# Pooled attention feeding a routed MoE: k and v read a batch further ahead, and all batches in one hand-ordered part

## The chip, the cores and the metric

One core of one Trainium2 chip runs the whole program. The metric is device microseconds for one execution; every number in the trace is in microseconds from the start of the profiled span unless it is marked ns. Engines are named as in the profile: PE (matmul), PEld (its weight load), DVE, ACT, POOL, and SP, which here issues DMAs and reads registers.

## The reference

Eight batches, eight heads, 576 tokens, head width 64. k and v are averaged over groups of 8 tokens (72 groups), then ordinary attention follows, and its output is the input of a mixture of experts with 4 groups of 4 experts, top 1 in each.

```python
k_p = k.reshape(B, H, Sp, 8, D).mean(axis=3)          # B=8 H=8 S=576 D=64, Sp=72
v_p = v.reshape(B, H, Sp, 8, D).mean(axis=3)
attn = softmax(q @ k_p.T / sqrt(D))                   # (B, H, S, 72)
x = (attn @ v_p).transpose(0, 2, 1, 3).reshape(4608, 512)
g_idx = argmax(x @ w_group); g_w = softmax(...)[g_idx]           # 4 groups
e_idx = argmax(x @ w_expert[g_idx]); e_w = softmax(...)[e_idx]   # 4 experts in the group
out[tok] = g_w * e_w * (relu(x[tok] @ w1[g, e]) @ w2[g, e])      # w1 512x1024, w2 1024x512
```

## The kernel before, in words

Work goes batch by batch. For each batch the kernel finds the expert that most of its tokens chose ("main expert"), and runs all 576 tokens through it; tokens of other experts are left to a loop behind the last batch. Products run in fp32r with both operands split into a high and a low half, so each up and each down product is three matmul passes. A batch has 16 up products (`m.up:f:half`, line 577, eight slices of the hidden width by two halves of the tokens, 12 matmuls each) and 14 pieces of down products (`m.down:z`, lines 606 and 617, 8 matmuls of 512 columns each).

Three batches are in flight. While batch b (`m`) runs its products, attention of b + 1 (`n`) and the pooling of b + 2 (`x`) are threaded between them. What the pieces do that matter here:

- `load_k`, `load_v` (lines 199 and 228): the reads of k and v of one batch from HBM, 1.31 MB each, on SP's queue, into the tiles `kv` and `vv`. Each of these has one buffer, so a read waits until the folds of the batch before have read it. v of the last batch goes in six DMAs instead of four, two of which overlap.
- `kr:0`, `kr:1` (line 263): k folded by sums over 8 tokens, on DVE, in place in `kv`, result in `kb`. `vr:0`, `vr:1` (line 282): the same for v on Pool, result in `v6`; `vm` (line 288) adds two short Pool operations.
- `load_qb` (line 255): q, 16 DMAs of small pieces on SP.
- `route`, `main_expert` (lines 427, 462): DVE finds the expert; SP reads its number into a register (line 475) and can only then issue `w.load` (line 541), four reads of 512 KB for w1 of the next batch. `w.load:2`, `m.load:2` are w2's. Tiles `sw` have four buffers.
- `cast` (ACT, line 554) makes a weight's high half, `lo` (Pool, line 560) the low half.
- `keep_x` (line 520): the attention output is stored to HBM where tokens are left over.
- LAST, the plan of the last batch, also places the left-over tokens (`l.step`, class Left). Its first step makes a triangle on Pool, copies it and a tile of ones on ACT (lines 691, 692), and has PE multiply with them (line 707).

The order of these pieces is written out by hand: START and FIRST (batch 0), SECOND (batch 1), STEADY (batches 2 to 6) and LAST (batch 7) are lists of pieces, and `run` calls them one after the other. Inside `tc.manual_schedule` each engine gets its instructions in the order of the calls. In the kernel before there is one such part for START, FIRST and SECOND, and one for each later batch. Where two parts meet, a scheduler merges their streams engine by engine.

The last batch begins:

```python
LAST = """
m.load:2:3 m.lo:1:2:v l.step l.step m.load:2:2 m.up:0:0 m.up:0:1 m.upd:0:1 m.upd:0:0 p.tail l.step ...
```

```python
nc.gpsimd.affine_select(out=tri, in_=ones, ...)
nc.scalar.copy(out=trir, in_=tri)      # line 691
nc.scalar.copy(out=onesr, in_=ones)    # line 692
...
nc.tensor.matmul(ps[:, 0:n], lhsT=lhs, rhs=lf[:, o:o + n], start=True, stop=True)   # line 707
```

Of the kernel before, what the change touches and what calls it, by code (L numbers as in the profile page):

```python
# [17 lines left out]
B, H, S, D = 8, 8, 576, 64  # L18
# [33 lines left out]
m.up:0:0 m.upd:0:0 n.qb:0 m.up:1:0 m.upd:1:0 m.split:1:2:p:2 m.load:2:2 a.count n.kt m.up:0:1 m.upd:0:1 a.keep_x m.split:1:3:p:2 m.load:2:3 m.up:1:1 m.upd:1:1 n.sc:0 n.mx:0 n.sb:0 n.qb:1 m.up:2:0 m.upd:2:0 n.su_:0 n.nm:0:p m.split:2:0:p:2 m.up:2:1 m.upd:2:1 n.sc:1 n.mx:1 n.sb:1 n.pt:0 n.qb:2  # L52
x.load_v m.up:3:0 m.upd:3:0 n.su_:1 n.nm:1:p m.split:2:1:p:2 m.up:3:1 m.upd:3:1 m.up:4:0 m.upd:4:0 n.sc:2 n.mx:2 n.sb:2 n.pt:1 n.qb:3 x.load_k m.split:2:2:p:2 m.up:4:1 m.upd:4:1 n.su_:2 n.nm:2:p m.up:5:0 m.upd:5:0 m.up:5:1 m.upd:5:1 n.sc:3 n.mx:3 n.sb:3 n.pt:2 n.qb:4
x.load_qb:0 x.load_qb:1 x.load_qb:2 x.load_qb:3 m.up:6:0 m.upd:6:0 n.su_:3 n.nm:3:p m.up:7:0 m.upd:7:0 n.av:0 n.avd:0 m.split:2:3:p:2 m.up:6:1 m.upd:6:1 n.sc:4 n.mx:4 n.sb:4 n.pt:3 m.up:7:1 m.upd:7:1 n.su_:4 n.nm:4:p m.down:0 n.pt:4 x.vr:0 m.down:1 x.vr:1 x.vm m.down:2 m.store:0 m.down:3 n.av:1 n.avd:1
m.down:4 x.kr:0 n.rt:0 n.rt:1 m.down:5 m.store:1 n.route_g n.route_e:p x.kr:1 m.down:6 m.down:7 x.qb:0 m.down:8 m.store:2 x.kt n.main_expert w.load:1:0 w.load:1:1 w.load:1:2 w.load:1:3 n.gates n.gm_ n.keep_x m.down:9 w.split:1:0:p:2 w.load:2:0
x.sc:0 x.mx:0 x.sb:0 m.down:10 x.qb:1 m.down:11 m.store:3 w.split:1:1:p:2 w.load:2:1 x.su_:0 x.nm:0:p m.down:12 w.cast:1:2 m.down:13 m.store:4 w.cast:1:3
"""
STEADY = """
m.up:0:0 p.tail m.upd:0:0 n.sc:1 n.pt:0 m.lo:1:2 m.load:2:2 m.up:0:1 n.mx:1 m.upd:0:1 m.up:1:0 n.sd:1 m.lo:1:3 m.load:2:3 m.upd:1:0 n.ex:1 m.up:1:1 m.cast:2:0 m.upd:1:1 n.su_:1 n.nm:1:p
m.up:2:0 m.upd:2:0 n.qb:2 m.lo:2:0 x.load_k x.load_v m.up:2:1 m.upd:2:1 n.pt:1 m.up:3:0 n.sc:2 m.upd:3:0 m.cast:2:1 m.lo:2:1 n.mx:2 m.up:3:1 m.upd:3:1 n.sd:2  # L60
m.up:4:0 m.upd:4:0 n.ex:2 m.up:4:1 m.upd:4:1 n.su_:2 n.nm:2:p x.load_qb:0 x.load_qb:1 m.up:5:0 m.upd:5:0 m.cast:2:2 m.lo:2:2 m.up:5:1 m.upd:5:1 n.pt:2
x.load_qb:2 x.load_qb:3 m.up:6:0 m.upd:6:0 m.up:7:0 m.cast:2:3 m.lo:2:3 m.upd:7:0 n.av:0 n.avd:0 m.up:6:1 m.upd:6:1
m.up:7:1 m.upd:7:1 n.av:1 n.rt:0 n.avd:1
m.down:0 n.rt:1 x.kr:0 m.down:1 x.kr:1 m.down:2 n.route m.down:3 m.down:4 m.down:5 n.main_expert w.load:1:0 w.load:1:1 w.load:1:2 w.load:1:3
x.qb:0 n.gates n.gm_ n.keep_x m.down:6 x.vr:0 x.kt m.down:7 x.sc:0 x.mx:0 x.sd:0 w.cast:1:0 w.lo:1:0 w.load:2:0 m.down:8 x.ex:0 x.qb:1 w.cast:1:1 w.load:2:1 m.down:9
x.su_:0 x.nm:0:p w.lo:1:1 m.down:10 x.vr:1 x.vm m.down:11 m.down:12 w.cast:1:2 m.down:13 w.cast:1:3
"""
LAST = """
m.load:2:3 m.lo:1:2:v l.step l.step m.load:2:2 m.up:0:0 m.up:0:1 m.upd:0:1 m.upd:0:0 p.tail l.step l.step l.step m.up:1:0 m.up:1:1 m.upd:1:0
# [7 lines left out]
MANUAL = {ET.PE, ET.SP, ET.DVE, ET.Activation, ET.Pool}  # L77

@with_exitstack
def attn_moe(ctx: ExitStack, tc: tile.TileContext, q, k, v, wg, we, w1, w2, out):  # L80
# [840 lines left out]
                nc.tensor.matmul(ps[:, 0:256], lhsT=ones, rhs=ones.unsqueeze(1).broadcast_to([128, 2, 128]), start=True, stop=True)  # L921

    left, top = Left(), Top()
    att = [Att(b) for b in range(B)] + [None] * 2
    moe = [Moe(a) if a else None for a in att]

    def run(plan, b):

        who = dict(a=att[b], m=moe[b], n=att[b + 1], w=moe[b + 1], p=moe[b - 1] if b else None, x=att[b + 2] if b + 2 < B else None, t=top, l=left)
        for piece in plan.split():  # L930
            name, *args = piece.split(":")
            who_, fn = name.split(".")
            if who[who_] is not None:
                getattr(who[who_], fn)(*[int(z) if z.isdigit() else z for z in args])

    with tc.manual_schedule(engines=MANUAL):
        run(START, 0)
        run(FIRST, 0)
        run(SECOND, 1)
    for b in range(2, B):  # L940
        with tc.manual_schedule(engines=MANUAL):
            run(LAST if b == B - 1 else STEADY, b)

    nit = nc.values_load(left.niti[0:1, 0:1], min_val=0, max_val=B * (NE + S // BS))
# [31 lines left out]
```

## Time and profile before

| what | value |
|---|---|
| median of 3 runs | 516.83 us (516.13 to 522.19) |
| profiled execution, its own time | 517.89 us |
| its span | 516.2 us |
| granted TensorE clock, mean | 0.998 of full speed |
| busy: PE, PEld, DVE, ACT, POOL | 503.1, 445.3, 328.7, 206.8, 255.2 us |
| DMA | 83.74 MB, mean 162 GB/s |

The span is the profiled program from its first to its last instruction; the execution's own time has about 1.7 us around it. Busy times of different engines overlap. A matmul's end is modelled, so a high busy share of PE says that it seldom stood still, not that every matmul ran at its best pace. An idle time of an engine is put down to the instruction of another engine that ended it; "issue" stands for a time in which the engine waited for nothing that the profile shows. DMA share is the mean busy share of 16 DMA engines and can come out slightly above 1 in short stretches.

### The profile page before, as it was taken

What the parts mean: (1) busy time and instruction counts of PE and PEld (TensorE: products, weight loads), DVE (VectorE), ACT (ScalarE), POOL (GpSimd) and SP (SyncE); (2) the same over time, 40 slices, a digit from 0 to 9 for tenths busy, and PEclk for the clock granted to TensorE, in tenths of its full rate; (3) what the DMA queues carried; (4) which work ended last, traced back from release to release, by engine and by line L of the source; (5) the groups of instructions that cost most, each with busy time, mean ns of one, the idle gap of its engine ahead of it and who ended that gap; (6) DMA issues with size and microseconds to landing.
All of it is one profiled execution on the core that took longest, in us unless ns stands there. A gap on an engine that the chain in (4) does not pass through costs nothing.

```text
span 516.2 us, 14897 instructions
## 1 busy us (share of the span) xinstructions
PE 503.1 (97%) x6085; PEld 445.3 (86%) x6085; DVE 328.7 (64%) x927; ACT 206.8 (40%) x385; POOL 255.2 (49%) x235
## 2 busy tenths in 40 slices
PE   8799999999999999999999999999999999989996
PEld 7698977998789988898889988898889988889876
DVE  6887877888376765485654766385664763268702
ACT  2454342454226441645235542454325551344212
POOL 2394766565418722785049641685138850422400
PEclk9999999999999999999999999999999999999999
DMA  8699299395248942788155961997345200743741
GB/s 278 191 272 195 54 265 258 76 241 108 52 131 247 244 77 103 225 244 139 28 198 162 249 90 44 336 336 134 56 150 196 76 2 20 237 160 123 265 165 57
DMA packets 118126, 83.74 MB, mean 162 GB/s; under 512 B 71034, under 2 KB 93818, under 8 KB 117800
## 3 DMA queue, kind: packets, MB, share of 16 engines
q1 hardware_dynamic: 113424, 75.70, 54.8%
q10 hardware_dynamic: 4600, 7.02, 3.9%
q8 instruction: 49, 0.80, 0.7%
q14 instruction: 21, 0.17, 0.1%
q0 software_dynamic: 32, 0.04, 0.0%
HBM read 77.31 MB, written 28.53 MB: 205 GB/s over the span
## 4 chain that ended last, share of the span: by engine, by line
PE 75%; DVE 9%; DMA 5%; POOL 3%; ACT 2%; issue 2%; SPq 1%; ACTq 1%; DVEq 0%; POOLq 0%
PE mm L577 29%; PE mm L606 26%; PE mm L617 4%; PE sc L393 4%; PE sc L333 3%; PE tp L411 3%; POOL w L560 2%; DMA sw<-in_moe_w_dram 2%; DMA vv<-in_v_dram 2%; DMA out_dram<-y 1%; PE mm L638 1%; DVE pT L379 1%; DVE s L365 1%; DVE ht L590 1%; DVE p L354 1%
## 5 line engine op out<-in xcount | busy, mean ns | idle before, releaser
L606 PE MATMUL mm<-w,ht 128*128 128x512 f32 x744 | 171.9, 384 | 0.0
L560 POOL TENSOR_TENSOR w<-sw,w 128x1024 fp32r<-128x1024 f32 (+2 forms) x87 | 148.9, 1729 | 43.5 <-ACT w L554 43.4
L606 PEld LDWEIGHTS mm<-w,ht 128*128 128x128 f32 x744 | 136.9, 189 | 21.1 <-issue 1.6
L577 PE MATMUL mm<-xb,w 128*128 128x288 f32 (+1 forms) x768 | 109.7, 295 | 1.0 <-issue 1.0
L577 PEld LDWEIGHTS mm<-xb,w 128*128 128x128 f32 x768 | 100.7, 189 | 5.7 <-ACT w L554 2.2
L577 PE MATMUL mm<-xa,w 128*128 128x288 f32 (+1 forms) x768 | 100.8, 284 | 3.0 <-DVE ht L590 1.4
L577 PEld LDWEIGHTS mm<-xa,w 128*128 128x128 f32 x768 | 95.5, 190 | 5.2 <-ACT ht L579 1.7
L579 ACT ACTIVATE ht<-mm 128x288 fp32r<-128x288 f32 (+2 forms) x128 | 51.9, 410 | 89.8 <-PE mm L577 88.1
L554 ACT CAST w<-sw 128x1024 fp32r<-128x1024 f32 x64 | 66.7, 1041 | 27.3 <-DMA sw<-in_moe_w_dram 24.5
L372 POOL TENSOR_TENSOR p<-p,su 128x864 f32<-128x864 f32 (+2 forms) x30 | 40.3, 1344 | 68.5 <-DVE su L367 53.3
L590 DVE SCALAR_TENSOR_TENSOR ht<-mm,ht 128x64 fp32r<-128x64 f32 (+4 forms) x192 | 37.7, 251 | 31.7 <-ACT ht L579 31.6
L611 ACT ACTIVATE y<-mm,gm 128x512 f32<-128x512 f32 x31 | 21.3, 686 | 68.1 <-PE mm L606 67.4
L512 POOL TENSOR_TENSOR mp<-oh,moh 128x80 f32<-128x80 f32 x8 | 2.9, 356 | 84.9 <-DVE moh L477 81.5
L359 ACT ACTIVATE p<-p 128x864 f32<-128x864 f32 (+2 forms) x30 | 23.4, 781 | 37.5 <-DVE p L354 29.8
L379 DVE STREAM_TRANSPOSE pT<-p 128x960 f32<-128x960 f32 (+2 forms) x30 | 29.2, 972 | 8.4 <-POOL p L372 7.8
L585 DVE SCALAR_TENSOR_TENSOR ht<-mm,ht 128x288 fp32r<-128x288 f32 (+1 forms) x64 | 27.0, 422 | 10.4 <-ACT ht L579 10.4
L365 DVE TENSOR_REDUCE s<-p 128x12 f32<-128x864 f32 (+2 forms) x30 | 25.8, 860 | 8.3 <-ACT p L359 8.3
L617 PE MATMUL mm<-w,ht 128*128 128x512 f32 x128 | 29.6, 381 | 0.0
L333 PEld LDWEIGHTS sc<-kT,qT 64*32 64x32 f32 x2176 | 23.7, 105 | 6.4 <-issue 3.5
L333 PE MATMUL sc<-kT,qT 64*32 64x72 f32 x2176 | 28.5, 230 | 0.5 <-DVE qT L319 0.3
L345 DVE TENSOR_REDUCE mx<-sc 128x12 f32<-128x864 f32 (+2 forms) x28 | 24.3, 868 | 5.5 <-PE sc L333 5.5
L393 PE MATMUL sc<-pT,v 32*64 32x288 f32 (+2 forms) x384 | 27.0, 409 | 0.2 <-DVE p L354 0.2
(213 smaller groups left out, 533.6 us busy)
## 6 DMA issues: line engine op xcount, KB each, us to landing
sw<-in_moe_w_dram SPq DMA_DIRECT2D x72, 512.0 KB
vv<-in_v_dram SPq DMA_DIRECT2D x27, 320.0 KB
q<-in_q_dram SPq DMA_DIRECT2D x112, 72.0 KB
kv<-in_k_dram SPq DMA_DIRECT2D x14, 512.0 KB
out_dram<-y ACTq DMA_DIRECT2D x23, 256.0 KB
xscr<-xa SPq DMA_DIRECT2D x5, 1152.0 KB
xscr<-xb SPq DMA_DIRECT2D x5, 1152.0 KB
pT<-xscr SPq DMA_DIRECT2D x4, 1152.0 KB
```

The source lines that it names most:

```text
L333: nc.tensor.matmul(ps[x][32 * g:32 * g + 32, SP * t:SP * t + SP], lhsT=s.qT[c][64 * x:64 * x + 64, g, 32 * t:32 * t + 32], rhs=s.kT[64 * x ...
L365: red(out=two[:, :, :, 0], in_=p.rearrange("p t (x s) -> p t x s", x=2), axis=AX.X, op=ALU.add)
L372: (nc.vector if eng == "v" else nc.gpsimd).tensor_tensor(out=p, in0=p, in1=bc(s.su[c][:, 0:w], SP), op=ALU.mult)
L379: nc.vector.transpose(out=s.pT[:, :, o:o + n].rearrange("p j (t i) -> p t j i", i=32), in_=probs[:, z:z + n // 32].rearrange("p t (j i) -> ...
L393: nc.tensor.matmul(banks[a][64 * x:64 * x + 64, 0:n], lhsT=s.v6[32 * a:32 * a + 32, 5 if x and i == 0 else j, :], rhs=s.pT[32 * a:32 * a + ...
L554: nc.scalar.copy(out=s.w[m, j][0], in_=raw)
L560: (nc.vector if eng == "v" else nc.gpsimd).tensor_tensor(out=wl[:, i:i + n], in0=s.raw[m, j][:, i:i + n], in1=wh[:, i:i + n].bitcast(F32), ...
L577: nc.tensor.matmul(ps[:, 0:n], lhsT=l[:, kc, fs], rhs=apart(s.a.xt[hf][:, r, kc]), start=(kc == 0 and i == 0), stop=(kc == 3 and i == 2))
L579: nc.scalar.activation(out=halves(ht[:, sl]), in_=joined(ps[:, 0:n]), func=AF.Relu)
L590: stt(out=ht[:, at:at + hi - lo], in0=ps[:, a, lo:hi], scalar=0.0, in1=ht[:, t + lo:t + hi].bitcast(F32), op0=ALU.max, op1=ALU.subtract)
L606: nc.tensor.matmul(ps, lhsT=s.ht[f][:, 640 * l + o:640 * l + o + 128], rhs=apart(s.w[2, f // 2][r][:, f % 2, :]), start=(i == 0), stop=(i ...
L617: nc.tensor.matmul(ps, lhsT=s.ht[f][:, 512:640], rhs=apart(s.w[2, f // 2][r][:, f % 2, :]), start=(i == 0), stop=(i == 15))
```

## The change

Two things change. First, the reads of k and v move a batch further ahead. A new letter `z` stands for batch b + 3 (`att` gets one more empty place at its end). In STEADY `x.load_k x.load_v` leave up product 2, and `z.load_v z.load_k` stand behind `x.kr:1` at the second piece of the down products; since `vv` has one buffer, Pool's `x.vr:0`, `x.vr:1` and `x.vm` move from the pieces 6 and 10 of the down products to their beginning, ahead of that read. SECOND gets `z.load_v z.load_k` behind its `x.kr:1`, while its own reads stay. Second, the batches 2 to 7 no longer have a part each: everything from START to LAST is one part.

```diff
 ... SECOND, its fourth line
-m.down:4 x.kr:0 n.rt:0 n.rt:1 m.down:5 m.store:1 n.route_g n.route_e:p x.kr:1 m.down:6 m.down:7 x.qb:0 m.down:8 m.store:2 x.kt n.main_expert w.load:1:0 ...
+m.down:4 x.kr:0 n.rt:0 n.rt:1 m.down:5 m.store:1 n.route_g n.route_e:p x.kr:1 z.load_v z.load_k m.down:6 m.down:7 x.qb:0 m.down:8 m.store:2 x.kt n.main_expert w.load:1:0 ...
 STEADY = """
 m.up:0:0 p.tail m.upd:0:0 n.sc:1 n.pt:0 m.lo:1:2 m.load:2:2 m.up:0:1 n.mx:1 m.upd:0:1 m.up:1:0 n.sd:1 m.lo:1:3 m.load:2:3 ...
-m.up:2:0 m.upd:2:0 n.qb:2 m.lo:2:0 x.load_k x.load_v m.up:2:1 m.upd:2:1 n.pt:1 m.up:3:0 n.sc:2 m.upd:3:0 m.cast:2:1 m.lo:2:1 n.mx:2 m.up:3:1 ...
+m.up:2:0 m.upd:2:0 n.qb:2 m.lo:2:0 m.up:2:1 m.upd:2:1 n.pt:1 m.up:3:0 n.sc:2 m.upd:3:0 m.cast:2:1 m.lo:2:1 n.mx:2 m.up:3:1 ...
...
-m.up:7:1 m.upd:7:1 n.av:1 n.rt:0 n.avd:1
-m.down:0 n.rt:1 x.kr:0 m.down:1 x.kr:1 m.down:2 n.route m.down:3 m.down:4 m.down:5 n.main_expert w.load:1:0 w.load:1:1 w.load:1:2 w.load:1:3
-x.qb:0 n.gates n.gm_ n.keep_x m.down:6 x.vr:0 x.kt m.down:7 x.sc:0 x.mx:0 x.sd:0 w.cast:1:0 w.lo:1:0 w.load:2:0 m.down:8 x.ex:0 x.qb:1 w.cast:1:1 w.load:2:1 m.down:9
-x.su_:0 x.nm:0:p w.lo:1:1 m.down:10 x.vr:1 x.vm m.down:11 m.down:12 w.cast:1:2 m.down:13 w.cast:1:3
+m.up:7:1 m.upd:7:1 n.av:1 n.rt:0 n.avd:1 x.vr:0
+m.down:0 n.rt:1 x.kr:0 x.vr:1 x.vm m.down:1 x.kr:1 z.load_v z.load_k m.down:2 n.route m.down:3 m.down:4 m.down:5 n.main_expert w.load:1:0 w.load:1:1 w.load:1:2 w.load:1:3
+x.qb:0 n.gates n.gm_ n.keep_x m.down:6 x.kt m.down:7 x.sc:0 x.mx:0 x.sd:0 w.cast:1:0 w.lo:1:0 w.load:2:0 m.down:8 x.ex:0 x.qb:1 w.cast:1:1 w.load:2:1 m.down:9
+x.su_:0 x.nm:0:p w.lo:1:1 m.down:10 m.down:11 m.down:12 w.cast:1:2 m.down:13 w.cast:1:3
...
-    att = [Att(b) for b in range(B)] + [None] * 2
+    att = [Att(b) for b in range(B)] + [None] * 3
...
-        who = dict(a=att[b], m=moe[b], n=att[b + 1], w=moe[b + 1], p=moe[b - 1] if b else None, x=att[b + 2] if b + 2 < B else None, t=top, l=left)
+        who = dict(a=att[b], m=moe[b], n=att[b + 1], w=moe[b + 1], p=moe[b - 1] if b else None, x=att[b + 2], z=att[b + 3], t=top, l=left)
...
         run(SECOND, 1)
-    for b in range(2, B):
-        with tc.manual_schedule(engines=MANUAL):
+        for b in range(2, B):
             run(LAST if b == B - 1 else STEADY, b)
```

## Rows read from the trace of the kernel before

**Rows 1.** Busy us of each engine, by stretch: batch 3, last batch (clock, DMA share, GB/s).

```profile
216.45:274.90 58.45, 57.50 (x711) 51.35 (x711) 36.65 (x97) 24.72 (x45) 28.27 (x21) 1.00 0.61 157
...
451.90:516.20 64.30, 58.55 (x500) 52.43 (x498) 33.77 (x119) 19.63 (x36) 13.07 (x16) 0.99 0.45 153
```

**Rows 2.** Waits of PE, then of SP's queue: us in total, times, longest.

```profile
PE mm L577 <- issue: 1.9, 2, 1.0
PE mm L577 <- DVE ht L590: 1.4, 1, 1.4
...
SPq L239 <- DMA vv<-in_v_dram: 9.5, 1, 9.5
```

**Rows 3.** Stretches of 4 us: PE, PEld, DVE, ACT, POOL busy; clock, DMA share, GB/s.

```profile
144.00:148.00 4.00, 4.00 (x23) 3.39 (x22) 3.79 (x9) 1.41 (x4) 0.97 (x1) 1.00 0.01 4
...
224.00:228.00 4.00, 4.00 (x34) 3.86 (x32) 3.64 (x12) 1.87 (x4) 1.98 (x3) 1.00 1.01 322
...
232.00:236.00 4.00, 3.05 (x25) 2.83 (x25) 2.95 (x7) 1.68 (x3) 0.60 (x1) 1.00 1.09 197
...
252.00:256.00 4.00, 4.00 (x23) 3.24 (x22) 1.93 (x7) 0.69 (x1) 0.00 (x0) 1.00 0.00 0
...
348.00:352.00 4.00, 3.01 (x25) 2.79 (x24) 1.84 (x6) 0.41 (x1) 3.11 (x2) 1.00 1.05 215
```

**Rows 4.** Timeline of SP's queue, batches 1 and 3: start, us, instruction.

```profile
141.30 6.16 SPq L658 DMA_DIRECT2D out_dram<-y  x2
...
149.22 2.88 SPq L548 DMA_DIRECT2D sw<-in_moe_w_dram  x4
...
225.05 1.89 SPq L235 DMA_DIRECT2D vv<-in_v_dram  x4
...
262.59 2.28 SPq L548 DMA_DIRECT2D sw<-in_moe_w_dram  x4
```

**Rows 5.** Timeline of POOL, batches 1 and 3.

```profile
129.01 1.29 POOL L273 TENSOR_TENSOR vv<-vv 128x512 f32<-128x512 f32 x1
...
135.22 0.66 POOL L291 TENSOR_TENSOR v<-v,share 128x64 f32<-128x64 f32 x2
...
154.10 5.08 POOL L560 TENSOR_TENSOR w<-sw,w 128x512 fp32r<-128x512 f32 x4 [4.67 <-ACT w L554]
...
242.38 2.37 POOL L560 TENSOR_TENSOR w<-sw,w 128x1024 fp32r<-128x1024 f32 x1 [1.94 <-ACT w L554]
```

**Rows 6.** Timeline of DVE, batch 0 (beside Pool) and batch 3 (alone).

```profile
90.17 1.55 DVE L273 TENSOR_TENSOR kv<-kv 128x768 f32<-128x768 f32 x1
...
250.99 0.95 DVE L273 TENSOR_TENSOR kv<-kv 128x768 f32<-128x768 f32 x1
...
255.05 0.33 DVE L438 TENSOR_REDUCE lg<-tp 128x80 f32<-128x160 f32 x1 [1.93 <-PE tp L435]
```

**Rows 7.** Timeline of PE and ACT where batches 2 and 4 begin.

```profile
157.06 1.50 PE L577 MATMUL mm<-xa,w 128*128 128x256 f32 x12
...
267.72 1.05 ACT L554 CAST w<-sw 128x1024 fp32r<-128x1024 f32 x1 [4.20 <-DMA sw<-in_moe_w_dram]
...
276.15 1.63 PE L577 MATMUL mm<-xa,w 128*128 128x288 f32 x12
```

**Rows 8.** Timeline where the last batch begins, and one earlier row of its part.

```profile
385.69 0.29 ACT L691 CAST v<-kb 128x128 fp32r<-128x128 f32 x1
...
448.02 3.62 PE L617 MATMUL mm<-w,ht 128*128 128x512 f32 x16
...
451.77 1.63 PE L577 MATMUL mm<-xa,w 128*128 128x288 f32 x12
...
453.88 0.58 ACT L622 COPY y<-mm 64x512 f32<-64x512 f32 x1
...
455.87 0.58 DVE L590 SCALAR_TENSOR_TENSOR ht<-mm,ht 128x144 fp32r<-128x144 f32 x3 [3.16 <-ACT ht L579]
...
456.61 1.71 PE L577 MATMUL mm<-xa,w 128*128 128x288 f32 x12 [1.43 <-DVE ht L590]
```

More of the change, by code (lines that the diff above doesn't have):

```diff
@@ L54 @@
 x.load_qb:0 x.load_qb:1 x.load_qb:2 x.load_qb:3 m.up:6:0 m.upd:6:0 n.su_:3 n.nm:3:p m.up:7:0 m.upd:7:0 n.av:0 n.avd:0 m.split:2:3:p:2 m.up:6:1 m.upd:6:1 n.sc:4 n.mx:4 n.sb:4 n.pt:3 m.up:7:1 m.upd:7:1 n.su_:4 n.nm:4:p m.down:0 n.pt:4 x.vr:0 m.down:1 x.vr:1 x.vm m.down:2 m.store:0 m.down:3 n.av:1 n.avd:1
-m.down:4 x.kr:0 n.rt:0 n.rt:1 m.down:5 m.store:1 n.route_g n.route_e:p x.kr:1 m.down:6 m.down:7 x.qb:0 m.down:8 m.store:2 x.kt n.main_expert w.load:1:0 w.load:1:1 w.load:1:2 w.load:1:3 n.gates n.gm_ n.keep_x m.down:9 w.split:1:0:p:2 w.load:2:0
+m.down:4 x.kr:0 n.rt:0 n.rt:1 m.down:5 m.store:1 n.route_g n.route_e:p x.kr:1 z.load_v z.load_k m.down:6 m.down:7 x.qb:0 m.down:8 m.store:2 x.kt n.main_expert w.load:1:0 w.load:1:1 w.load:1:2 w.load:1:3 n.gates n.gm_ n.keep_x m.down:9 w.split:1:0:p:2 w.load:2:0
 x.sc:0 x.mx:0 x.sb:0 m.down:10 x.qb:1 m.down:11 m.store:3 w.split:1:1:p:2 w.load:2:1 x.su_:0 x.nm:0:p m.down:12 w.cast:1:2 m.down:13 m.store:4 w.cast:1:3
@@ L59 @@
 m.up:0:0 p.tail m.upd:0:0 n.sc:1 n.pt:0 m.lo:1:2 m.load:2:2 m.up:0:1 n.mx:1 m.upd:0:1 m.up:1:0 n.sd:1 m.lo:1:3 m.load:2:3 m.upd:1:0 n.ex:1 m.up:1:1 m.cast:2:0 m.upd:1:1 n.su_:1 n.nm:1:p
-m.up:2:0 m.upd:2:0 n.qb:2 m.lo:2:0 x.load_k x.load_v m.up:2:1 m.upd:2:1 n.pt:1 m.up:3:0 n.sc:2 m.upd:3:0 m.cast:2:1 m.lo:2:1 n.mx:2 m.up:3:1 m.upd:3:1 n.sd:2
+m.up:2:0 m.upd:2:0 n.qb:2 m.lo:2:0 m.up:2:1 m.upd:2:1 n.pt:1 m.up:3:0 n.sc:2 m.upd:3:0 m.cast:2:1 m.lo:2:1 n.mx:2 m.up:3:1 m.upd:3:1 n.sd:2
 m.up:4:0 m.upd:4:0 n.ex:2 m.up:4:1 m.upd:4:1 n.su_:2 n.nm:2:p x.load_qb:0 x.load_qb:1 m.up:5:0 m.upd:5:0 m.cast:2:2 m.lo:2:2 m.up:5:1 m.upd:5:1 n.pt:2
 x.load_qb:2 x.load_qb:3 m.up:6:0 m.upd:6:0 m.up:7:0 m.cast:2:3 m.lo:2:3 m.upd:7:0 n.av:0 n.avd:0 m.up:6:1 m.upd:6:1
-m.up:7:1 m.upd:7:1 n.av:1 n.rt:0 n.avd:1
-m.down:0 n.rt:1 x.kr:0 m.down:1 x.kr:1 m.down:2 n.route m.down:3 m.down:4 m.down:5 n.main_expert w.load:1:0 w.load:1:1 w.load:1:2 w.load:1:3
-x.qb:0 n.gates n.gm_ n.keep_x m.down:6 x.vr:0 x.kt m.down:7 x.sc:0 x.mx:0 x.sd:0 w.cast:1:0 w.lo:1:0 w.load:2:0 m.down:8 x.ex:0 x.qb:1 w.cast:1:1 w.load:2:1 m.down:9
-x.su_:0 x.nm:0:p w.lo:1:1 m.down:10 x.vr:1 x.vm m.down:11 m.down:12 w.cast:1:2 m.down:13 w.cast:1:3
+m.up:7:1 m.upd:7:1 n.av:1 n.rt:0 n.avd:1 x.vr:0
+m.down:0 n.rt:1 x.kr:0 x.vr:1 x.vm m.down:1 x.kr:1 z.load_v z.load_k m.down:2 n.route m.down:3 m.down:4 m.down:5 n.main_expert w.load:1:0 w.load:1:1 w.load:1:2 w.load:1:3
+x.qb:0 n.gates n.gm_ n.keep_x m.down:6 x.kt m.down:7 x.sc:0 x.mx:0 x.sd:0 w.cast:1:0 w.lo:1:0 w.load:2:0 m.down:8 x.ex:0 x.qb:1 w.cast:1:1 w.load:2:1 m.down:9
+x.su_:0 x.nm:0:p w.lo:1:1 m.down:10 m.down:11 m.down:12 w.cast:1:2 m.down:13 w.cast:1:3
 """
```

## The prediction, made before the changed kernel was run

> **What bounds the kernel now.** I read the table of the batches first, then PE's waits, then the DMA share in steps of 4 us, and last the timeline of each queue that the edits touch. A steady batch is 58.45 us long, of which PE works 57.50 [rows 1]. Busy is not proof that PE is at its peak, so I looked for what PE waits for: in the whole run the waits of its up products are two of about 1 us each named "issue" and one of 1.4 us on DVE [rows 2]. There is no wait for k, for v or for the sums over them. So whatever the edits do to k and v, the time that they can give back from batch 2 on is about 3 us, and the question is rather what they may cost.
>
> The DMA table shows where the traffic lies. Up products of batch 3, 224 to 228: share 1.01, 322 GB/s; 232 to 236: share 1.09, and PE busy only 3.05 of 4.00 us. First down products, 252 to 256: nothing moves [rows 3]. k and v are now issued in the crowded stretch (v's four DMAs at 225.05), and would go to the empty one [rows 4].
>
> **1. The reads of k and v, steady batches.** Removed from up product 2, added behind kr:1 at the first down products: seven DMAs, 4 x 320 KB and 2 x 512 + 256 KB, 2.62 MB. Each tile has one buffer, so v's read waits for vr:1 on Pool and k's for kr:1 on DVE. When? Pool ends its last weight step at 242.38 + 2.37 = 244.75 [rows 5] and has nothing then. The moved vr:0, vr:1 and vm together took 135.22 + 0.66 - 129.01 = 6.9 us back to back in batch 1 [rows 5], so in batch 3's place they end at 251.6, vr:1 itself at about 251.0. SP issues v from there (1.9 us [rows 4]), k from about 253. At the 322 GB/s of [rows 3] 2.62 MB need 8.1 us: landed by about 260. Queued behind them on SP: the register read of the main expert and the four weight loads, issued at 262.59 [rows 4]. They stay where they are, with 2 us to spare. If that cover goes, the weights come up to 8.1 us later; the first cast runs at 267.72, its Pool difference (2.4 us) ends near 271.2, and the up products start at 276.15 and use it 1 us later [rows 5, 7]: about 6 us of slack, so even then 2 us a batch. Taken: 0, bounds 0 and +2 a batch; no gain, since nothing waited for k or v.
>
> For the last batch v is read in six DMAs, of which the sixth waits on SP for the landing of the fifth: 9.5 us in the crowded stretch [rows 2]. In the empty one it is some 4 us (1.31 MB at 322 GB/s). With the old 9.5 the weights behind would be late by less than their slack. Taken: 0.
>
> **2. What leaves the crowded stretch.** Of PE's two "issue" waits, one falls in 232 to 236, the other in 348 to 352, where PE is busy 3.01 of 4.00 us and 215 GB/s move at share 1.05 [rows 3]. I read them as PE short of instructions while the DMA engines are full; the rows don't prove it. The q loads stay, and at 232 to 236 they are in the mix (share 1.09 but only 197 GB/s, small packets). At 348 to 352 they are not: they stood on SP behind the 9.5 us wait of the last v [rows 2]. So the later wait, in k's and v's own traffic, should go, -1.0 us; the earlier should stay. Bounds: both go, -1.9; as many new ones come, +2. The Trainium skill ("Runtime: NRT & Kernel Launch", "Instruction fetch mechanics") says that crossing an instruction block is mostly hidden. No row here shows a fetch, so the trace decides only that waits exist under full DMA queues; by that rule this term would be 0.
>
> **3. v's sums on Pool.** Removed: vr:0 ahead of batch 4's first weight difference, vr:1 and vm among the next ones. Nothing on PE waits for Pool there [rows 2], so the 6.9 us give no time. Added: Pool work beside DVE's folding of k. Where they meet in the first batch, DVE's 128x768 fold took 1.55 us; alone it takes 0.95 [rows 6]. After k's fold DVE idles 1.93 us before the routing at 255.05 [rows 6]. Pool is done by 251.6, and the fold starts about 1.5 us (an estimate) ahead of the step at 250.99, so at most 2.1 us overlap; at the rate 1.55 to 0.95 that costs 1.3 us or less and disappears in the idle time. Taken: 0; bounds 0 and +1 a batch, and then only if the slack of part 1 is gone too. The Trainium skill ("SBUF — State Buffer", "Who interferes with whom") speaks against the move: a Vector tensor_tensor with both inputs in SBUF and a GpSimd operation that reads SBUF shut each other out for a whole instruction. The 1.55 us agree with a block of part of an instruction; a full block of 2.1 us would pass the idle 1.93 by 0.2 us, and end in the slack of the weights.
>
> **4. The same reads in batch 1.** Here z.load_v and z.load_k stand behind kr:1 and ahead of the third store and the weights, whose issue is at 149.22; from 144 to 148 DMA moves 4 GB/s [rows 3, 4]. vr:1 is done long before, about 135 [rows 5], but SP reaches the reads only behind the second store, whose issue is at 141.30 [rows 4], and most of k waits longer, for kr:1. 8.1 us from 142 are 150, so the weights are some 1 us late (bounds 0.5 and 1.5). The first weight's two Pool differences end at 154.10 + 2.5 = 156.6, and PE's first product starts at 157.06 and needs them 1 us on [rows 5, 7]: slack 1.4 us. Taken: +0.3, bounds 0 and +1.5.
>
> **5. One part.** Parts are merged by the scheduler where an engine is idle, in order only within a part. The clearest row: the two ACT copies with which the last batch's placing starts (L691, L692) ran at 385.69, in batch 5, though the last part's own products start at 451.77 [rows 8]. In one part they stand behind everything of batch 6 on ACT, and PE's two products of that step (L707) stand ahead of the first up product and read them. By the hand's order: L617 ends at 448.02 + 3.62 = 451.64; then L622 0.58 (in the old merge it came only at 453.88), the last cast 1.05 [rows 7], two copies of 0.29: 453.7. The two products take 0.3: first up product at 454.1 instead of 451.77. Up 0:0 and 0:1, about 1.5 us each: 457.1. Its ACT eviction with the gaps around it 0.6 (an estimate by L622's 0.58), DVE's L590 0.58: up 1:0 starts near 458.5. Before, it starts at 456.61, since it then waited 1.43 us for L590, which the old merge had pushed back [rows 8]. So the loss is +1.9 us, not the 2.3 at the first product. The last batch loses 5.75 of 64.30 us of PE in all, end of the kernel included [rows 1], so nothing behind takes the shift up. Bounds: 0, if the copies run early all the same, and +2.4. At the other seams PE's order is the hand's already; the relu of batch 2's first product will stand behind a weight cast, which is inside the bounds of part 4.
>
> **Sum.** 517.89 us (profiled: span 516.2 and 1.7 around it) - 1.0 + 0.3 + 1.9 = 519.1. The median of the three runs lies 1.1 us lower, 516.83, so on its scale +1.2 is 518.0 us.
>
> **Rivals.**
> A. Both ways of reading are hidden, and the seam costs nothing either: then only the "issue" waits count, 516.83 - 1.0 = 515.8, and 514.9 if both go. For it: no wait for k or v anywhere [rows 2]. Against it: the order of L617, L622, cast and copies is plain arithmetic. That the change does nothing at all is the upper end of this, 516.8.
> B. Weights late, slower than before. Place: the SP ring at the first down products of batches 1 to 4. If vr:1 ends late or the reads run at 200 GB/s (13 us) instead of 322, the four weight loads queue behind k and v. It decides when the reads land later than 262.6 plus the slack of 6, about 268.5. Price up to 2 us in each of four batches: 518.0 + 4 to 8 = 522 to 526. Against it: the stretch is empty [rows 3], and 11 us lie between vr:1's end and the issue of the weights.
> C. The "issue" waits are not k's and v's doing, and move with the code: term 2 is 0 to +2: 519.0 to 521. For it: the four batches 2 to 5 read k and v alike, and only two show such a wait [rows 2]. By the sentence of the Trainium skill in part 2 it would be 519.0.
>
> **How the numbers follow.** Forecast 0.45 (517 to 519), A 0.32 (514.9 to 516.9), C 0.13 (519 to 521), B 0.10 (521 to 527, 0.03 of it more). A run of this kernel tells from no change what goes beyond 2%, 10.3 us: 506.5 and 527.2. Faster would need 10 us where PE waits for about 3: 0.01. Slower over 2%: B at its worst, 0.03. Same: 0.96. The range takes all of A but a thin edge for the scatter of runs (the lowest lies 0.7 under the median), forecast and C, and the start of B: 514.2 to 521.8.
>
> **What would show it.** In the changed profile: DMA 224 to 236 without the 300 GB/s, and the empty stretch at the first down products filled; no "issue" wait of PE near 349; vr on Pool right behind the last weight difference of the up products; weight loads at the same distance from the routing; and in the last batch PE waiting about 2 us for ACT (L692) ahead of L707, while the wait on L590 shrinks or stays near 1 us. Wrong it would be if the batches 2 to 6 changed their period of about 58.5 us, if a weight cast waited over 6 us longer for its DMA, or if L691 and L692 still ran early.

## The result and the profile after

The changed kernel is slower: 522.56 us (median of 19 runs, 521.1 to 525.71) against 518.08 us for the kernel before (19 runs beside it, 516.13 to 522.19). The ratio is 1.0086, with a 95% interval of 1.0068 to 1.0103. The forecast was 518.0 us, 0.2% above the median that it started from, and its range ended at 521.8. Of the 4.6 us between the forecast and the measured median 1.25 are the base: the 19 runs of the kernel before lie that much above the 516.83 us of the three runs from which the forecast started. The profiled execution of the changed kernel took 521.11 us (span 519.3, mean granted clock 1.000), the one of before 517.89 (span 516.2, clock 0.998). Each experiment below has runs of the kernel before beside it on its chip (median 518.55 us for the first four, 517.71 for the next ones, 518.33 for the last two); its ratio is worked out from all of these and need not equal the quotient of the two medians. Executions of one kernel fall into a faster and a slower state, and the medians and ratios here are those of the faster one (two of the ten runs with the reads behind the weights were in the slower).

To see where 3.1 us of span come from I took one row of PE's timeline that occurs once in each batch, the route transposes (L435), and subtracted its starts from one another. Every profiled execution of this study is a row of the table; the issue waits are those of PE on nothing that the profile shows, in the up products from batch 1 on (the reads alone have one more of 0.4 us in batch 0).

| kernel | batch 1 to 2 | 2 to 3 | 3 to 4 | 4 to 5 | 5 to 6 | issue waits |
|---|---|---|---|---|---|---|
| before | 54.19 | 59.86 | 58.65 | 59.91 | 58.65 | 2 |
| after | 58.57 | 58.64 | 58.64 | 58.64 | 58.64 | 0 |
| before, a second time | 54.18 | 59.63 | 58.64 | 59.68 | 58.64 | 2 |
| one part alone | 55.13 | 58.65 | 58.64 | 58.64 | 58.64 | 0 |
| reads alone | 58.22 | 58.64 | 58.65 | 58.64 | 58.64 | 0 |
| no reads in batch 1 | 55.38 | 58.65 | 58.64 | 58.65 | 58.65 | 0 |
| v of batch 1 earlier | 57.77 | 58.64 | 58.64 | 58.65 | 58.64 | 0 |
| reads behind the weights | 62.84 | 58.65 | 58.64 | 58.64 | 58.64 | 0 |
| no reads in batch 1, early copies | 55.45 | 58.64 | 58.64 | 58.65 | 58.64 | 0 |
| the same, a second time | 55.57 | 58.64 | 58.65 | 58.64 | 58.65 | 0 |
| one part, early copies | 55.23 | 60.34 | 58.65 | 58.64 | 58.64 | 1 |
| no reads in batch 1, early copies, later cast | 54.33 | 58.65 | 58.64 | 58.65 | 58.65 | 0 |

So the change costs 4.4 us between batches 1 and 2, gives 1.2 and 1.3 back in two later batches, and from the transposes of batch 6 to the end of the span it costs 1.5 (85.91 against 84.45): 4.4 - 2.5 + 1.5 = 3.4, less the 0.2 by which its first transposes came earlier (140.26 against 140.49), is the 3.1 of the spans.

The first loss, in the timeline of the changed kernel where batch 1 ends (start, us, engine, instruction, and in brackets the idle time before it with what ended it):

```profile
141.54 1.86 SPq L235 DMA_DIRECT2D vv<-in_v_dram  x4
...
146.24 0.91 SPq L207 DMA_DIRECT2D kv<-in_k_dram  x2
147.19 0.47 SPq L208 DMA_DIRECT2D kv<-in_k_dram  x1
...
149.25 3.12 SPq L548 DMA_DIRECT2D sw<-in_moe_w_dram  x4
...
156.84 1.04 ACT L554 CAST w<-sw 128x1024 fp32r<-128x1024 f32 x1 [9.22 <-DMA sw<-in_moe_w_dram]
...
157.94 1.16 PE L577 MATMUL mm<-xa,w 128*128 128x256 f32 x8 [0.93 <-ACT w L554]
...
159.29 0.49 PE L577 MATMUL mm<-xa,w 128*128 128x256 f32 x2 [0.19 <-POOL w L560]
...
160.52 0.49 PE L577 MATMUL mm<-xa,w 128*128 128x256 f32 x2 [0.74 <-POOL w L560]
...
173.24 1.21 PE L333 MATMUL sc<-kT,qT 64*32 64x72 f32 x96 [0.73 <-DVE qT L319]
```

The weights are issued at 149.25, as before [rows 4]. Their first cast waits 9.22 us for its load and starts 7.6 us after the issue. In the kernel before it started 3.8 us after the issue:

```profile
152.98 1.04 ACT L554 CAST w<-sw 128x1024 fp32r<-128x1024 f32 x1 [5.15 <-DMA sw<-in_moe_w_dram]
```

PE, which before ran its first product at 157.06 without a break [rows 7], now waits for the cast and twice for Pool's low halves. The stretches of 4 us show why (PE, PEld, DVE, ACT, POOL busy; clock, DMA share, GB/s):

```profile
144.00:148.00 4.00, 4.00 (x23) 3.40 (x22) 3.79 (x10) 1.42 (x4) 0.97 (x1) 1.00 1.05 213
148.00:152.00 4.00, 4.00 (x110) 3.29 (x109) 3.58 (x12) 0.00 (x0) 0.71 (x2) 1.00 1.06 321
152.00:156.00 4.00, 4.00 (x21) 3.49 (x20) 0.98 (x2) 0.00 (x0) 0.00 (x0) 1.00 1.06 358
...
232.00:236.00 4.00, 4.00 (x120) 3.75 (x120) 2.96 (x6) 1.77 (x3) 4.00 (x3) 1.00 0.53 86
...
256.00:260.00 4.00, 4.00 (x23) 3.24 (x22) 2.73 (x12) 0.69 (x1) 0.00 (x0) 1.00 1.07 220
...
348.00:352.00 4.00, 4.00 (x120) 3.75 (x119) 3.75 (x7) 1.75 (x3) 4.00 (x3) 1.00 0.46 78
```

From 144 to 156 the DMA engines are full, where before 4 GB/s moved from 144 to 148 [rows 3]. In the steady batch the same reads fill 256 to 260, and 232 to 236 and 348 to 352, where PE stood still before [rows 3], are at a share of 0.53 and 0.46 with PE busy throughout. The same products lie 2.9 and 1.6 us later in the changed kernel; in the 4 us behind these stretches the share is 0.66 and 0.72, and PE is busy there too. The waits of PE in the whole run:

```profile
PE tp L707 <- ACT v L692: 2.0, 1, 2.0
PE mm L577 <- DVE ht L590: 1.7, 2, 0.9
PE mm L577 <- POOL w L560: 1.6, 3, 0.7
...
PE mm L577 <- ACT w L554: 0.9, 1, 0.9
PE sc L333 <- DVE qT L319: 0.7, 1, 0.7
```

No wait of its up products is named "issue" any more [rows 2]; in their place stand waits for the late weights and one for L692. The last is in the timeline of the last batch:

```profile
449.66 3.62 PE L617 MATMUL mm<-w,ht 128*128 128x512 f32 x16
...
453.31 0.58 ACT L622 COPY y<-mm 64x512 f32<-64x512 f32 x1 [1.16 <-PE mm L617]
453.80 1.04 ACT L554 CAST w<-sw 128x1024 fp32r<-128x1024 f32 x1
...
454.95 0.30 ACT L692 CAST v<-ones 128x128 fp32r<-128x128 f32 x1
455.29 0.56 PE L707 MATMUL tp<-loh,v 128*128 128x320 f32 x2 [2.02 <-ACT v L692]
455.69 1.63 PE L577 MATMUL mm<-xa,w 128*128 128x288 f32 x12
```

L691 and L692, which ran in batch 5 before [rows 8], stand behind L622 and the cast. The steady reads behave as wanted; the rows that answer to [rows 4 to 6] are, in batch 3 of the changed kernel:

```profile
247.65 1.27 POOL L273 TENSOR_TENSOR vv<-vv 128x512 f32<-128x512 f32 x1
...
253.21 0.92 POOL L286 TENSOR_TENSOR v<-vv 128x192 f32<-128x192 f32 x1
...
254.16 1.75 SPq L235 DMA_DIRECT2D vv<-in_v_dram  x4
...
254.79 1.05 DVE L273 TENSOR_TENSOR kv<-kv 128x768 f32<-128x768 f32 x1
...
257.98 0.33 DVE L438 TENSOR_REDUCE lg<-tp 128x80 f32<-128x160 f32 x1 [0.95 <-PE tp L435]
...
265.51 2.25 SPq L548 DMA_DIRECT2D sw<-in_moe_w_dram  x4
...
268.97 1.05 ACT L554 CAST w<-sw 128x1024 fp32r<-128x1024 f32 x1 [2.51 <-DMA sw<-in_moe_w_dram]
```

This batch lies 2.93 us later in the changed kernel (its L435 at 257.47 against 254.54). Pool's sums end with the read of v at once behind them; the fold of k, slowed by Pool, eats about half of DVE's idle time (0.95 left of 1.93); and the weights leave at the same distance from the routing, 8.04 us behind L435 against 8.05.

### The profile page after: what moved, and what is told of

Its sections match the earlier page's. It is cut to its first block, busy times and chain, and to the rows that moved or that the text cites. A ratio compares the mean times of both kernels' runs of the same rounds, so it can differ in the third digit from the quotient of the medians.

```text
span 519.3 us, 14878 instructions
## 1 busy us (share of the span) xinstructions
PE 503.2 (97%) x6085; PEld 445.1 (86%) x6085; DVE 331.2 (64%) x927; ACT 206.4 (40%) x385; POOL 258.5 (50%) x235
## 4 chain that ended last, share of the span: by engine, by line
PE 78%; DVE 10%; DMA 4%; ACT 3%; POOL 3%; issue 2%; SPq 1%; ACTq 0%; DVEq 0%; POOLq 0%
PE mm L606 29%; PE mm L577 29%; PE sc L393 4%; PE mm L617 4%; PE sc L333 4%; PE tp L411 3%; POOL w L560 2%; DMA sw<-in_moe_w_dram 2%; DMA vv<-in_v_dram 1%; ACT w L554 1%; PE mm L638 1%; DVE mx L345 1%; DVE p L354 1%; DVE ht L590 1%; DVE ht L585 1%
## 5 line engine op out<-in xcount | busy, mean ns | idle before, releaser
L577 PE MATMUL mm<-xb,w 128*128 128x288 f32 (+1 forms) x768 | 109.4, 294 | 0.1
L577 PE MATMUL mm<-xa,w 128*128 128x288 f32 (+1 forms) x768 | 101.5, 284 | 4.5 <-DVE ht L590 1.7
L577 PEld LDWEIGHTS mm<-xb,w 128*128 128x128 f32 x768 | 100.6, 189 | 4.5 <-ACT w L554 2.2
L577 PEld LDWEIGHTS mm<-xa,w 128*128 128x128 f32 x768 | 95.6, 190 | 7.6 <-POOL w L560 2.2
L617 PE MATMUL mm<-w,ht 128*128 128x512 f32 x128 | 29.6, 381 | 0.0
```

The source lines that it names most:

```text
L577: nc.tensor.matmul(ps[:, 0:n], lhsT=l[:, kc, fs], rhs=apart(s.a.xt[hf][:, r, kc]), start=(kc == 0 and i == 0), stop=(kc == 3 and i == 2))
L617: nc.tensor.matmul(ps, lhsT=s.ht[f][:, 512:640], rhs=apart(s.w[2, f // 2][r][:, f % 2, :]), start=(i == 0), stop=(i == 15))
```

## The experiments

**The reads of batch 1 left out.** Theory: the reads that the change adds in batch 1 take the DMA engines from the weights of batch 2. Here k and v of batch 4 are read in batch 2 at up product 2, as before; all else is the changed kernel.

```diff
-... x.kr:1 z.load_v z.load_k m.down:6 ...
+... x.kr:1 m.down:6 ...
...
+THIRD = STEADY.replace("n.qb:2 m.lo:2:0 ", "n.qb:2 m.lo:2:0 x.load_k x.load_v ")
...
-            run(LAST if b == B - 1 else STEADY, b)
+            run(LAST if b == B - 1 else THIRD if b == 2 else STEADY, b)
```

> The changed kernel without the two reads added to batch 1: k and v of batch 4 are read in batch 2 at up product 2, as before; all else stays changed. Theory (the reads of batch 1 stand ahead of batch 2's weights on SP and cost 4.2 us there): batch 2 starts as in the kernel before, ratio to before near 1.000 (0.998 to 1.002). Rival (the loss comes from the one part, or from Pool and DMA work moved in the steady batches): ratio stays at 1.0086.

Measured: 519.35 us, ratio 1.0011 [0.9988, 1.0034]; the period of batch 1 to 2 falls from 58.57 to 55.38. The reads of batch 1 cost 3.2 us, and without them the loss against before can no longer be measured. The 1.2 us that stay (55.38 against 54.19) must come from elsewhere.

**The reads without the one part.** The changed plans, each batch with a part of its own as before.

```diff
-        for b in range(2, B):
+    for b in range(2, B):
+        with tc.manual_schedule(engines=MANUAL):
             run(LAST if b == B - 1 else STEADY, b)
```

> The changed plans, but each batch from 2 on in a part of its own, as before. Theory (4.2 us at the start of batch 2, of which about 1.5 us is the first eviction standing behind a late weight cast by the hand's order, and 1.5 us at the last batch): both parts of the order go, 3 us less, ratio 1.002 to 1.004. Rival (the order costs nothing at batch 2, only the late weights do): 1.5 us less, ratio 1.0055.

Measured: 520.15 us, ratio 1.0014 [0.9994, 1.0034]. From the transposes of batch 6 to the end 84.24 us: the loss at the last batch is gone with the one part. Batch 1 to 2 stays at 58.22, so on top of late weights the order adds only 0.35, where the theory had about 1.5 and its rival nothing. The ratio lies below what either gave: by the ratios of this kernel and of the changed one the one part costs 3.7 us, by the profiles 0.35 and 1.7. What may fill the gap is said below.

**The one part without the reads.** The kernel before with its `with` for each batch taken away.

```diff
-    for b in range(2, B):
-        with tc.manual_schedule(engines=MANUAL):
+        for b in range(2, B):
             run(LAST if b == B - 1 else STEADY, b)
```

> The kernel before with the one part alone; all reads and v's sums stay where they were. Theory: PE waits about 2 us for the two ACT copies at the last batch, net 1.5 to 2 us, ratio 1.003 to 1.004, and the two waits named issue stay. Rival (the whole loss is the order by hand): 1.0086. Second rival (the merge of parts was worth nothing): 1.000.

Measured: 520.08 us, ratio 1.0032 [1.0009, 1.0055]; batch 1 to 2 55.13, 0.9 more than before; L707 waits 2.0 us for L692, as in the changed kernel. So by itself the order costs about 1 us at the start of batch 2, and its wait at the last batch. The issue waits were expected to stay and did not. In its last batch the trace shows a second price of that wait, first in its timeline:

```profile
452.41 0.56 PE L707 MATMUL tp<-loh,v 128*128 128x320 f32 x2 [2.02 <-ACT v L692]
452.81 2.24 PE L577 MATMUL mm<-xa,w 128*128 128x288 f32 x12
454.84 2.74 PE L577 MATMUL mm<-xb,w 128*128 128x288 f32 x12
```

and then in its stretches of 4 us:

```profile
448.00:452.00 4.00, 2.39 (x12) 1.75 (x10) 1.45 (x1) 2.62 (x4) 4.00 (x4) 1.00 0.86 211
452.00:456.00 4.00, 3.59 (x19) 3.59 (x20) 0.89 (x2) 0.77 (x3) 4.00 (x3) 0.71 0.67 249
456.00:460.00 4.00, 3.08 (x21) 2.85 (x20) 1.94 (x7) 0.78 (x2) 2.47 (x11) 0.86 0.37 86
```

Behind the wait the granted clock falls to 0.71 and 0.86 of full speed, so for part of these stretches to its lower level (1.2 in place of 2.4 GHz), and the next two up products take 2.24 and 2.74 us in place of 1.63 each: 1.7 us more.

**Early copies.** The kernel without the reads of batch 1, and the first step of the placing (triangle and both copies) called in batch 6, before the last batch's queue on ACT; a `yield` behind the step's setup ends it there. SIXTH is the plan of batch 6.

```diff
+SIXTH = STEADY.replace("n.rt:1 x.kr:0", "n.rt:1 l.step x.kr:0")
...
             nc.gpsimd.iota(s.colf, ...)
+            yield
```

> As e1, and the first step of the placing (the triangle and the two ACT copies) is called in batch 6 at the first down products, its products stay in the last batch. Theory: no PE wait at the last batch, both issue waits gone: 518.1 - 2.5 = 515.6 us, ratio 0.995. Rival (the two issue waits went by chance, not with k's and v's traffic): they come back somewhere, ratio 1.000.

Measured: 516.48 us, ratio 0.995 [0.9924, 0.9977]. The wait for L692 is gone, L707 runs right behind L617, and the kernel is faster than the kernel before and the changed one. Run once more (below), it came to 0.9964.

**The kernel before a second time**, to see whether its issue waits recur.

> The kernel before, unchanged, for a second profile. If the two issue waits of PE belong to its order of instructions, both come back at the same places (batches 3 and 5, periods of 59.9 us beside 58.6). If they come and go from execution to execution, they are elsewhere or gone, all periods 58.6.

Measured: they recur in the same two batches; the page of waits has "PE mm L577 <- issue: 1.5, 2, 0.8", and the periods are 59.63 and 59.68. So the same places show them in both executions.

**v of batch 1 read earlier.** The read of v stands right behind Pool's `x.vm`, ahead of the first store, so that v moves in the empty stretch; k must wait for `kr:1`.

```diff
-... x.vr:1 x.vm m.down:2 m.store:0 ...
+... x.vr:1 x.vm z.load_v m.down:2 m.store:0 ...
...
-... x.kr:1 z.load_v z.load_k m.down:6 ...
+... x.kr:1 z.load_k m.down:6 ...
```

> The changed kernel, with batch 1's added read of v moved ahead, right behind v's sums and ahead of the first store, into the stretch where DMA is idle; k's read stays behind kr:1. Theory (bytes of k and v still ahead of the weights on SP's ring at their issue delay them): 1.31 MB less are ahead, the first cast of batch 2's weights waits about 2 to 3 us less, ratio 1.003 to 1.005. Rival (it is the contention of any two loads at that time, or the order): ratio stays at 1.0086.

Measured: 521.09 us, ratio 1.0062 [1.0035, 1.0089], batch 1 to 2 57.77. Half a miss: v is out of the way, but the first cast still waits 8.44 us for its load, only 0.8 less than in the changed kernel. Even 1.31 MB issued 3 us ahead of the weights make them late: with k alone 3.6 of the 4.4 us stay.

**Both reads behind the weights.** The same two reads, behind the four weight reads in SP's order.

```diff
-... x.kr:1 z.load_v z.load_k m.down:6 ...
+... x.kr:1 m.down:6 ...
...
-... w.load:1:2 w.load:1:3 n.gates ...
+... w.load:1:2 w.load:1:3 z.load_v z.load_k n.gates ...
```

> The changed kernel, with both added reads of batch 1 moved behind the four weight reads, everything else changed as it was. Theory: the weights land as in the kernel before (first cast after about 5 us of waiting), ratio about 1.001 as without the reads. Rival (the reads slow the weights whatever their place in the queue, since all share 16 engines): ratio 1.005 or more.

Measured: 523.9 us, ratio 1.0104 [1.0065, 1.0143], batch 1 to 2 62.84: a miss, and no better than the changed kernel. The profiled execution took 527.06 us, 3.1 above this median, so its 62.84 is on the high side. The timeline where its batch 2 starts:

```profile
149.13 2.69 SPq L548 DMA_DIRECT2D sw<-in_moe_w_dram  x4
151.92 2.81 SPq L235 DMA_DIRECT2D vv<-in_v_dram  x4
...
152.81 1.05 ACT L554 CAST w<-sw 128x1024 fp32r<-128x1024 f32 x1 [5.06 <-DMA sw<-in_moe_w_dram]
...
173.30 1.04 ACT L554 CAST w<-sw 128x1024 fp32r<-128x1024 f32 x1 [3.91 <-DMA sw<-in_moe_w_dram]
...
176.02 1.24 PE L333 MATMUL sc<-kT,qT 64*32 64x72 f32 x96 [4.04 <-DVE qT L319]
```

Its stretches of 4 us:

```profile
156.00:160.00 4.00, 4.00 (x117) 3.64 (x116) 0.23 (x1) 2.18 (x3) 2.98 (x4) 1.00 1.09 222
160.00:164.00 4.00, 2.87 (x23) 2.62 (x21) 0.68 (x1) 2.60 (x5) 4.00 (x3) 1.00 1.08 204
164.00:168.00 4.00, 2.70 (x17) 2.33 (x18) 3.92 (x8) 0.65 (x3) 2.21 (x1) 1.00 1.02 279
...
176.00:180.00 4.00, 3.98 (x106) 3.84 (x107) 2.83 (x6) 0.36 (x1) 3.10 (x2) 0.63 0.55 91
```

The first cast is on time, 3.7 us behind its issue. But the reads now hold up what follows: a cast of w2 waits 3.91 us for its load (the first of w2's loads is issued at 165.80, in the kernel before at 156.65), ACT's queue stands behind it, and PE waits 4.04 us for the scores of the next batch, with the clock at 0.63 behind that. The Trainium skill ("DMA: Bandwidth & Descriptors", "Queues, rings and completion order") says that a DMA engine takes the descriptors of a ring in their order. The wait of the first cast, 5.06 us with the weights in front and 9.22 behind, agrees with it. By that order alone this kernel would be about as fast as the one without the reads. It is not: the DMA share is above 1.0 from 156 to 168, and 2.62 MB more find no room on either side of the weights.

**One part with early copies, reads unmoved.** The kernel before in one part, with the early copies; this takes the price of the order away and leaves the reads as they were.

```diff
-    for b in range(2, B):
-        with tc.manual_schedule(engines=MANUAL):
-            run(LAST if b == B - 1 else STEADY, b)
+        for b in range(2, B):
+            run(LAST if b == B - 1 else SIXTH if b == B - 2 else STEADY, b)
```

> The kernel before in one part, with the first step of the placing called in batch 6 (all reads and v's sums unmoved). If the moved reads give nothing and the order everything, it is as fast as the same with the reads moved in the steady batches: ratio 0.995. If the moved reads give what the issue waits cost, 2 us: ratio 0.999.

Measured: 517.19 us, ratio 0.998 [0.9957, 1.0003], with one issue wait of 1.4 us (period 60.34). Beside the 0.995 and 0.9964 of the kernel whose steady reads are moved this leaves 0.8 to 1.6 us for the moved reads. The intervals overlap and the runs were on different chips, so the runs do not show this gain; the period that holds the wait shows 1.7.

**The late relu of batch 2.** Why does one part cost 1 us at the start of batch 2 when the weights are on time? In its order the last cast of the first up weights stands ahead of the relu behind the first up product on ACT. The kernel with early copies, with this cast moved behind that relu, and beside it on the same chip the kernel with early copies again.

```diff
-... m.down:13 m.store:4 w.cast:1:3
+... m.down:13 m.store:4
...
-THIRD = STEADY.replace(...)
+THIRD = STEADY.replace(...).replace("m.upd:0:0 ", "m.upd:0:0 m.cast:1:3 ", 1)
```

> The kernel without the reads of batch 1 and with the early copies, in which the last cast of the first up weights of batch 2 stands behind the eviction of the first up product instead of ahead of it on ScalarE. Theory (one part costs 0.9 to 1.3 us at the start of batch 2 because that cast, which waits for its load, stands ahead of the relu): the relu behind the first up product runs right after it, as in the kernel before, the period of batch 1 to 2 falls from 55.45 to 54.2 to 54.6, the score product's wait for qT and that for L592 there shrink, and the ratio to the kernel before is 0.992 to 0.994. Rival (VectorE's own order there holds the scores and the late relu costs nothing): the period stays at 55.3 to 55.5 and the ratio at 0.995.

> The kernel without the reads of batch 1 and with the early copies once more, as the neighbour of the kernel with the later cast on the same chip: 0.994 to 0.997 of the kernel before, a period of batch 1 to 2 of 55.3 to 55.6, no issue wait of TensorE.

Measured: 515.46 us, ratio 0.9943 [0.992, 0.9965], batch 1 to 2 54.33; the neighbour 516.5 us, 0.9964 [0.9944, 0.9984], 55.57. The timeline of the neighbour, and then of the kernel with the later cast:

```profile
157.42 1.50 PE L579 MATMUL mm<-xa,w 128*128 128x256 f32 x12
...
160.73 1.03 ACT L556 CAST w<-sw 128x1024 fp32r<-128x1024 f32 x1
161.79 0.71 ACT L581 ACTIVATE ht<-mm 128x256 fp32r<-128x256 f32 x2
```

```profile
157.11 1.50 PE L579 MATMUL mm<-xa,w 128*128 128x256 f32 x12
...
160.25 0.38 ACT L581 ACTIVATE ht<-mm 128x256 fp32r<-128x256 f32 x1
160.53 1.04 ACT L556 CAST w<-sw 128x1024 fp32r<-128x1024 f32 x1
```

With the later cast the relu (L581) runs ahead of the cast, 1.2 us earlier in its batch, and the period falls by 1.24 us to within 0.14 of the kernel before. The ratios alone don't separate the two kernels, since their intervals overlap; the periods do. This is the fastest version of the study, 0.6% below the kernel before.

## Why the prediction was wrong, point by point

**Failed step: part 4, the added reads in batch 1**, sized at +0.3 with an upper bound of 1.5, measured at 4.4 (58.57 against 54.19). Its place was named; the arithmetic failed in three spots. It let 2.62 MB flow from 142 at 322 GB/s and land at 150; but from 144 to 148, with v in front and k issued only at 146.24, the engines moved 213 GB/s at share 1.05. The 322 was read from 224 to 228 of the kernel before, where k, issued at 223.51, stood in front of v; with v in front the rate is lower (last section). It said itself that k waits for `kr:1` and then didn't count that: k is issued at 146.24 to 147.7, just ahead of the weights. And "the weights are some 1 us late" turned out to be 3.8 us at the first cast (156.84 - 149.25 = 7.6 us behind the issue, before 152.98 - 149.22 = 3.8). The slack of 1.4 us that was claimed covered little of it. The experiments split the 4.4, but not into a plain sum: without the order the reads cost 4.0 (58.22 against 54.19) and with it 3.2; the order costs 0.9 without the added reads and the moved sums, 1.2 without the added reads and 0.35 on top of them. That fits a PE that waits for the later of two things and not for both. The order's share of 0.35 to 1.2 was put "inside the bounds of part 4" without a price, though the prediction had the mechanism: the relu stands behind a weight cast. The later cast takes it away.

**Part 5, one part: right in mechanism and nearly in size.** In the time frame of before (1.64 us earlier, by L617) L707 ran at 453.65 (predicted 453.8), up 0:0 at 454.05 (454.1), up 1:0 at 458.37 (458.5). Two steps of its sum are rounded unevenly: 451.64, 0.58, 1.05 and twice 0.29 make 453.85, not 453.7, and with products of 1.5 us up 1:0 would start at 458.3, not 458.5. The loss would then be 1.7 us; 458.37 against 456.61 is 1.8. From the last batch to the end it cost 1.5 in the profile instead of 1.9. What the step lacked is the clock: it fell behind this wait in two of the five profiled kernels that have it (the one part alone, 0.71; the reads behind the weights, 0.57 from 460 to 464), and not there in any of the seven profiled executions without the wait. Removing it gave 2.9 us in the runs (519.35 to 516.48; 2.4 to 3.2 by the ratios of the two runs of the faster kernel), up to twice the 1.5 of the profile. The clock is a candidate for the rest, for the gap of the reads alone above, and for the 1.45 us by which the changed kernel's median lies above its profiled execution, in which the clock stayed at 1.00 there; only one execution of it was traced, so that part stays open.

**Part 2, the issue waits: right in sign, too small.** Forecast -1.0, measured -2.5: both waits went, not only the one near 349, and each was worth 1.2 to 1.3 us of period in the first profile of the kernel before (1.0 in the second). The reasoning that q's small packets would keep the earlier one failed: 232 to 236 fell to share 0.53. Rival C, that these waits move with the code, holds in part. In the seven kernels with the steady reads moved none is seen from batch 1 on, in eight profiled executions, with and without the one part; so moving the reads is enough. With the reads unmoved, two recur in the same batches, one appears 3 us later in batch 3 (1.4 us, in the one part with early copies), and the one part alone has none although its DMA share is 1.07 from 232 to 236 and from 348 to 352. Full DMA engines are thus not sufficient, and the order or the place of the code matters too, which of the two no run tells; what PE lacks in those waits stays open. In the changed kernel either edit may have removed them, and that part 2 has the right sign rests on the seven kernels and not on its reason. The sentence of the Trainium skill in part 2 ("Runtime: NRT & Kernel Launch", "Instruction fetch mechanics") would have made this term 0. The 2.5 us of period speak against it only if the waits are fetches, which no row shows.

**Parts 1 and 3, the steady batches: right.** In the time frame of before v is issued at 251.2 (predicted 251.0) and k at 254.1 (253). DVE's 128x512 fold took 1.28 us beside Pool in place of 0.68 alone, its 128x768 fold 1.05 in place of 0.95; in all it lost 1.0 us of its 1.93 of idle time, below the 1.3 allowed and far from a full block of 2.1, and the next batch's weights were not later. The last v's wait for its fifth DMA fell from 9.5 to 5.8 us (predicted some 4; at the 220 GB/s seen from 256 to 260 1.31 MB take 6.0) and cost nothing that a period shows. Rival B had the right mechanism, weights late behind k and v on SP's ring, but in the wrong place: batches 2 to 4 have 11 us of cover and kept their period, while batch 1 has no such cover and paid once.

**Sum.** In the terms of the profile: forecast +0.3 - 1.0 + 1.9 = +1.2, measured +4.4 - 2.5 + 1.5 = +3.4. Part 2 erred to the good side by 1.5, part 5 by 0.4, and part 4 to the bad side by 4.1; that the errors partly cancel is luck.

## What to carry to other kernels

A read that is moved ahead in a loop is paid for in the pass that starts the pipeline, where it is added and nothing leaves; ask there, in that pass's own rows, when its last byte can be issued and which load on the critical path comes next on the same queue. Count the bytes of the whole stretch before changing their order: where the DMA engines are full on both sides, another order only moves the wait. And where separately scheduled parts are joined into one hand order, list what the scheduler had pulled ahead (here two small copies and a relu, together 2.7 us of profile) and place it by hand.

## What was not expected of the hardware

A full DMA share doesn't tell the rate. In batch 3 of the changed kernel the four reads of v, 320 KB into 32 partitions each, are issued first (254.16), k's behind them (257.06), and the weights only at 265.51:

```profile
258.00:260.00 2.00, 2.00 (x10) 1.76 (x11) 1.72 (x10) 0.27 (x1) 0.00 (x0) 1.00 1.04 211
...
262.00:264.00 2.00, 2.00 (x12) 1.79 (x11) 0.41 (x2) 0.64 (x1) 0.00 (x0) 1.00 1.03 386
```

From 258 to 260, with v in front, 211 GB/s moved; from 262 to 264, when v's 1.31 MB were through and k was moving (0.64 of 0.77 MB on SP's queue, the rest a store on ACT's), 386, at the same share. k's reads fill 128 partitions at a time; that this makes the difference fits, but no run separates it from the size of the read. PE's issue waits recur in the same batches of the same kernel from one execution to the next. And a wait of PE of 2.0 us was followed by a granted clock of 0.71, so partly at the lower of its two levels, in one kernel, and of 1.00 in the changed one with the same wait.
